# The order of small steps around TensorE in a two-layer attention and gMLP kernel: keys' sum, block sums, early transposes, row statistics

## The chip, the cores and the metric

The kernel runs on one core of a Trainium2 chip. TensorE (PE) multiplies matrices and writes into PSUM banks; VectorE (DVE), ScalarE (ACT) and GpSimd (POOL) do the element-wise work; SyncE (SP) issues all DMA transfers. Each engine works through its own instructions in the order in which the program issued them, and semaphores hold an instruction back until what it needs is there. The metric is the device time of one execution in microseconds, the median of several runs.

## The reference

Four residual blocks follow each other on x (2048 rows of 512), all in float32: attention A, mixer B, A, B, with the same weights in both layers.

```python
def _A_ref(x, wqkv, wo):                      # H = 32 heads of 16
    q, k, v = ...                             # from x @ wqkv
    phi = lambda t: jnp.where(t > 0, t + 1, jnp.exp(t)) + 1e-6
    pq, pk = phi(q), phi(k)
    kv = jnp.einsum("bhsd,bhse->bhde", pk, v)
    z = jnp.einsum("bhsd->bhd", pk)           # the keys' sum
    num = jnp.einsum("bhqd,bhde->bhqe", pq, kv)
    den = jnp.einsum("bhqd,bhd->bhq", pq, z)[..., None] + 1e-6
    return (num / den)... @ wo
...
def _B_ref(x, w_in, w_sp, b_sp, w_out):
    z = _gelu(jnp.einsum("bsd,df->bsf", x, w_in))
    z1 = z[..., :Fh]                          # Fh = 896
    z2 = _layernorm(z[..., Fh:], axis=-1)
    g = jnp.einsum("ts,bsf->btf", w_sp, z2) + b_sp[None, :, None]
    return jnp.einsum("bsf,fd->bsd", z1 * g, w_out)
...
x = x + _A_ref(_layernorm(x, axis=-1), A_wqkv, A_wo)
x = x + _B_ref(_layernorm(x, axis=-1), B_w_in, B_w_sp, B_b_sp, B_w_out)
...                                           # and both once more
```

## The kernel before, in words

The rows are cut into 16 tiles of 128. Every operand of a matmul is split into a high part (fp32r, made by an ACT copy, `high`, L119) and a low part (the rest, made by a DVE subtraction, `low`, L122), and each product is three matmuls: high by high, high by low, low by high (`mm3`, L133 to L135). So PE reads a low part only at its third matmul.

Per layer there are four stages, in this order:

- **P1** goes through the tiles i and makes keys and queries. Step s of `P1.run` works on several tiles at once: it loads x(s+3), takes row statistics of tile s+2 (`ln_a`: `stats` on DVE, L196 and L198, and three small POOL instructions, L200 to L203, of which the last makes `nb`), normalises tile s+2 on ACT (`ln_b`, L209), turns tile s (`T_high`, `T_low`), multiplies K of tile s-1 and Q of tile s-1 on PE, applies phi on ACT and DVE (`K_phi`, `Q_phi`, L327 to L329), splits x and the keys of tile s-1 (`xsplit`; `K_split`, L340 and L341) and accumulates G of tile s-2 (`Gmm`). Q of the last six tiles is put off (`late`) into the following stage. A side queue splits one piece of a further weight per step. `Turn` turns a tile in one of two ways: by four PE transposes into a PSUM bank (L221), for the tiles in `by_pe` (0, 1, 2 in the first layer, 10 to 15 in both), or by a store of the tile as `xt` to DRAM and a reload with another layout (`turn.load`), followed by a DVE transpose within 32x32 blocks (L260).
- **The keys' sum** z is accumulated in `K_split` by a POOL add of two SBUF tiles (L346).
- **The block sums** (`Sums`) belong to a later stage, which multiplies by w_sp with seven block products instead of eight and needs sums of blocks of w_sp. `tick` stores the sums of the tick before, issues loads for the next, and has POOL add twice (L788). There are 32 ticks, in the first layer alone: six in steps 2 to 7 of P1, the others in P2 and P4.
- **transition** and **P2**: the small products of attention; then per tile the product of pq and z on POOL (`a`, L567), the denominators (`a2_den`, L579 to L581), their product with pq (`a2_mul`, L588, and in the first tiles a copy on ACT, L240), turning (`b_high`, `b_low`), the matmul `c`, the residual add and row statistics (`c2`), store and normalise (`c3`), turning again (`d_high`, `d_low`), and the products of the mixer (`e`, `f`). Steps 1 to 4 turn by PE and carry the deferred Q.
- **P4** multiplies by w_sp and by w_out; `o(i)` makes output tile i and `zsplit(i)` its operand. In the first layer `join` puts the start of the next layer's P1 beside it: loads, statistics, and the splits of wk and wq.

There is no planner: the order is the one written out in the code. SBUF tiles come from queues of fixed slots: 22 pages of 128x512 floats (`pages`), larger `quads` and `bigs`, and eight PSUM banks. `get` takes the slot that has been free longest (`popleft`, L41), `put` adds one at the end (L50). A slot is given back when the instruction that reads it last is issued, and the next one to write it waits on a semaphore for that reader.

Of the kernel before, what the change touches and what calls it, by code (L numbers as in the profile page):

```python
# [13 lines left out]
OP = mybir.AluOpType  # L14
# [5 lines left out]
NT = S // P  # L20
# [51 lines left out]
def mixer_kernel(ctx: ExitStack, tc: tile.TileContext, x_in, wqkv, wo_d, win1_d, win2_d, wsp_d, bsp_d, wout_d,  # L72
# [192 lines left out]
    class P1:  # L265
# [71 lines left out]
        def K_split(self, i):  # L337
            r = self.r.pop(i)
            h, l = pages.get(PAGE, F32R), pages.get(PAGE, F32R)
            nc.scalar.activation(h, r, AF.Copy, bias=PHI_EPS)  # L340
            nc.vector.scalar_tensor_tensor(l, r, PHI_EPS, h.bitcast(F32), op0=OP.add, op1=OP.subtract)  # L341
            self.pk[i] = (h, l)
            if i == 0:
                self.zacc = r
            else:
                nc.gpsimd.tensor_tensor(self.zacc, self.zacc, r, op=OP.add)  # L346
                pages.put(r)

        def Q(self, i):
            self.qb = self.proj(i, self.wq)  # L350
# [78 lines left out]
        def run(self, sums):  # L429
            side = deque()  # L430
            for w in (self.wv, self.wo, self.win2):
                side.extend([w] * len(w.pieces))
            side[0].fetch()
            ND = NT - DEFER
            for s in range(1, NT + 2):
                self.loadx(s + 3)
                self.turn.load(s + 1)
                if 2 <= s < NT:
                    self.T_high(s)
                if s == 1:  # L440
                    if not self.kb:
                        self.K(0)
                    self.K(1)
                elif 2 < s <= NT:
                    self.K(s - 1)
                self.ln_a(s + 2)
                if 2 <= s < NT:
                    self.T_low(s)
                if s <= NT:
                    self.K_phi(s - 1)  # L450
                if s <= ND:
                    self.Q(s - 1)
                if s == NT + 1:
                    self.late()
                if s <= NT:
                    self.xsplit(s - 1)
                    self.K_split(s - 1)
                self.ln_b(s + 2)
                if s <= ND:
                    self.Q_phi(s - 1)  # L460
                if s >= 2:
                    self.Gmm(s - 2)
                if s == NT + 1:
                    self.late_phi()
                if self.L == 0 and s == 2:
                    sums.slots = Sheets(bigs, 2)
                if self.L == 0 and 2 <= s < 8:
                    sums.tick(s < 7)
                if self.L == 0 and s == 8:
                    sums.store()  # L470
                    sums.slots.close()
                    sums.slots = pages
                if side:
                    side.popleft().piece()
                if side:
                    side[0].fetch()
            while side:
                side.popleft().piece()


    def transition(p1, p2):
        wv, wo = p1.wv, p1.wo
        zh, zl = pages.get(PAGE, F32R), pages.get(PAGE, F32R)
        za = p1.zacc
        nc.vector.tensor_scalar(za, za, NT * PHI_EPS, None, op0=OP.add)
        split(zh, zl, za, True)
        pages.put(za)
        p1.late()
        p1.wk.free()
        g = (quads.get([P, 4, 512], F32R), quads.get([P, 4, 512], F32R))  # L490
        for c in range(4):
            split(g[0][:, c, :], g[1][:, c, :], p1.G[c])
            banks.put(p1.G[c])
        zb = banks.get(PAGE)
        nc.tensor.matmul(zb, ones, zh, start=True, stop=False)
        nc.tensor.matmul(zb, ones, zl, start=False, stop=True)
        pages.put(zh, zl)
        p2.zbc = pages.get(PAGE)
        nc.scalar.activation(feats(p2.zbc, True), feats(zb, False), AF.Copy)
        banks.put(zb)  # L500
        p2.a(0)
        p1.late_phi()
        p2.win1.fetch()
        p2.win1.fetch()
        p2.zeps = small.tile([P, 32], F32, name="zeps", bufs=1)
        nc.vector.tensor_reduce(p2.zeps, p2.zbc.rearrange("p (h d) -> p h d", d=16), axis=mybir.AxisListType.X,
                                op=OP.add)
        nc.vector.tensor_scalar(p2.zeps, p2.zeps, PHI_EPS, PHI_EPS, op0=OP.mult, op1=OP.add)

        p2.a2_den(0)  # L510
        m = pages.get([P, 4, P])
        for q in range(4):
            b = banks.get([P, P])
            s = slice(q * P, (q + 1) * P)
            for c in range(4):
                mm3(b, (wv.h[:, c, s], wv.l[:, c, s]), (g[0][:, c, s], g[1][:, c, s]), c == 0, c == 3)
            nc.vector.tensor_mul(m[:, q, :], b, mask)
            banks.put(b)
        kvh, kvl = pages.get([P, 4, P], F32R), pages.get([P, 4, P], F32R)
        for q in range(0, 4, 2):  # L520
            split(kvh[:, q:q + 2, :], kvl[:, q:q + 2, :], m[:, q:q + 2, :])
        pages.put(m)
        quads.put(*g)
        wv.free()
        p2.a2_mul(0)
        p2.a(1)
        p1.late()
        p2.a2_den(1)
        p2.W2 = (quads.get([P, 4, 512], F32R), quads.get([P, 4, 512], F32R))
        for q in range(4):  # L530
            b = banks.get(PAGE)
            mm3(b, (kvh[:, q, :], kvl[:, q, :]), (wo.h[:, q, :], wo.l[:, q, :]), True, True)
            split(p2.W2[0][:, q, :], p2.W2[1][:, q, :], b)
            banks.put(b)
            if q == 1:
                p2.b(0)
        pages.put(kvh, kvl)
        wo.free()
        p2.a(2)
        p1.late_phi()  # L540
        p2.a2_mul(1)
        p1.late()
        p2.a(3)
        p2.a2(2)
        p1.late_phi()


    class P2:
# [69 lines left out]
        def c2(self, i):  # L618
            x = self.x[i]
            nc.vector.tensor_add(x, x, self.cb)  # L620
            banks.put(self.cb)
            self.ms[i] = stats(x, 1)

        def c3(self, i):
            x = self.x.pop(i)
# [75 lines left out]
        def run(self, sums):  # L701
            w1 = self.win1
            for s in range(1, NT + 3):
                self.loadx(s + 1)
                self.qturn.load(s + 1)
                if s in self.qturn.by_pe:
                    self.c(s - 1)
                    self.b_high(s)
                    self.c2(s - 1)
                    self.b_low(s)  # L710
                    if s >= 2:
                        self.d_high(s - 2)
                        self.d_low(s - 2)
                    self.p1.late()
                    self.c3(s - 1)
                    self.a2(s + 2)
                    self.p1.late_phi()
                    self.a(s + 3)
                else:
                    if s < NT:  # L720
                        self.b_high(s)
                    self.a2_den(s + 2)
                    if s < NT:
                        self.b_low(s)
                    if s <= NT:
                        self.c(s - 1)
                        self.c2(s - 1)
                    if s == NT:
                        quads.put(*self.W2)
                        pages.put(self.zbc)  # L730
                    self.a2_mul(s + 2)
                    late = s - 2 in self.xturn.by_pe
                    if late:
                        self.d_high(s - 2)
                        self.d_low(s - 2)
                    if s <= NT:
                        self.c3(s - 1)
                    self.a(s + 3)
                    if s <= NT + 1 and not late:
                        self.d_high(s - 2)  # L740
                        self.d_low(s - 2)
                if s >= 4:
                    self.e4(s - 4)
                self.xturn.load(s - 1)
                if s >= 3:
                    self.e(s - 3)
                    self.e2(s - 3)
                    self.e3(s - 3)
                self.f()
                self.f()  # L750
                self.fq.extend(self.fnext)
                self.fnext = []
                w1.piece(True)
                w1.fetch()
                if s > 7:
                    sums.tick()
                if s >= NT + 1:
                    self.p4.fetch(s - NT - 1)
# [53 lines left out]
    class P4:  # L812
# [243 lines left out]
        def join(self, i, nxt):  # L1056
# [9 lines left out]
            if i in (11, 12):  # L1066
                nxt.turn.load(i - 11)
            if 10 <= i < 14:
                nxt.wk.piece()
                nxt.wq.piece()  # L1070
            if i == 14:
                nxt.T(0)
            if i == 15:
# [47 lines left out]
```

## Time and profile before

| | us |
|---|---|
| median of 3 runs | 1407.29 (1407.14 to 1407.45) |
| the profiled execution | 1407.07 |
| its span in the profile | 1405.3 |
| PE busy | 1394.3 (99%) |
| DVE busy | 889.5 (63%) |
| ACT busy | 572.7 (41%) |
| POOL busy | 405.8 (29%) |

All times below are microseconds from the start of the span. In the first layer P1 runs from about 10 to 132, the transition to about 152, P2's first steps follow; the second layer's P1 begins at about 707 and its P2 at about 848. A row of the timeline gives start, duration, engine, line, operation, the tiles written and read, and in brackets the idle time before it and what ended that. A PE matmul's end is modelled and overlaps the next, so spacing of starts says when PE stood still.

### The profile page before, as it was taken

The page shows a single profiled execution, that of the slowest core. Times are in us where ns is not written, and L with a number is a line of the kernel's source. Part 1 is how long each engine was busy: PE and PEld are TensorE (multiplying, and loading weights), DVE is VectorE, ACT ScalarE, POOL GpSimd, SP SyncE. Part 2 cuts the span into 40 slices and gives each one's busy share as a digit, 9 for nine tenths or more (in the row PEclk, how much of TensorE's full clock was granted, in tenths as well). Part 3 has the DMA queues.
Part 4 walks back from the last instruction along what each step waited for, and adds up shares of the span by engine and source line. Part 5 has one row for each costly group of instructions (what it writes and reads, how often), then busy time and mean ns, then how long its engine had stood idle before and what let it go on. Part 6 is the DMA issues. An engine that isn't in the chain of part 4 may idle for free.

```text
span 1405.3 us, 17490 instructions
## 1 busy us (share of the span) xinstructions
PE 1394.3 (99%) x6318; PEld 1167.0 (83%) x6318; DVE 889.5 (63%) x1263; ACT 572.7 (41%) x871; POOL 405.8 (29%) x490
## 2 busy tenths in 40 slices
PE   9999999999999999999999999999999999999998
PEld 7788888888888888888888888888888888888887
DVE  7876786753587666583578767766415466666632
ACT  5665544434322332351366655444333233333420
POOL 3843244544366002040023334432100030022300
PEclk9999999999999999999999999999999999999999
DMA  5831156766887433443644212555335344434432
GB/s 198 258 117 46 56 177 213 258 226 204 326 299 265 133 121 136 167 163 120 210 127 142 61 38 93 183 177 163 114 119 158 105 165 134 130 120 169 152 112 90
DMA packets 134390, 219.39 MB, mean 156 GB/s; under 512 B 11552, under 2 KB 44064, under 8 KB 134304
## 3 DMA queue, kind: packets, MB, share of 16 engines
q1 hardware_dynamic: 134304, 218.28, 47.5%
q8 instruction: 49, 0.80, 0.2%
q14 instruction: 37, 0.30, 0.1%
HBM read 153.49 MB, written 64.75 MB: 155 GB/s over the span
## 4 chain that ended last, share of the span: by engine, by line
PE 93%; DVE 2%; ACT 1%; DMA 1%; POOL 1%; issue 1%; SPq 0%; ACTq 0%; DVEq 0%; POOLq 0%
PE bank L135 18%; PE bank L134 18%; PE bank L133 18%; PE bank L908 13%; PE bank L910 13%; PE bank L909 13%; PE bank L221 1%; DMA pg<-in_wqkv_dram 1%; DVE qd L122 0%; DMA pg<-in_x_dram 0%; DVE st L196 0%; DVE pg L588 0%; ACT z_q L328 0%; ACT pg L209 0%; ACT z_q L327 0%
## 5 line engine op out<-in xcount | busy, mean ns | idle before, releaser
L908 PE MATMUL bank<-qd,pg 128*128 128x512 f32 x800 | 311.3, 389 | 0.0
L910 PE MATMUL bank<-qd,pg 128*128 128x512 f32 x800 | 311.2, 389 | 0.0
L909 PE MATMUL bank<-qd,pg 128*128 128x512 f32 x800 | 311.2, 389 | 0.0
L847 DVE TENSOR_TENSOR qd<-qd,qd 128x1024 fp32r<-128x1024 f32 x112 | 151.9, 1356 | 175.6 <-ACT qd L846 175.4
L846 ACT ACTIVATE qd<-qd 128x1024 fp32r<-128x1024 f32 x112 | 118.5, 1058 | 215.8 <-PE bank L910 195.5
L935 POOL TENSOR_TENSOR bg<-bg,pg 128x512 f32<-128x512 f32 x56 | 85.5, 1562 | 408.8 <-DVE bg L962 195.5
L910 PEld LDWEIGHTS bank<-qd,pg 128*128 128x128 f32 x800 | 150.2, 188 | 31.3
L908 PEld LDWEIGHTS bank<-qd,pg 128*128 128x128 f32 x800 | 150.1, 188 | 31.3 <-DVE bg L953 0.2
L909 PEld LDWEIGHTS bank<-qd,pg 128*128 128x128 f32 x800 | 150.2, 188 | 31.2
L135 PE MATMUL bank<-qd,pg 128*128 128x512 f32 x384 | 150.7, 392 | 3.0 <-DVE pg L122 3.0
L200 POOL TENSOR_SCALAR rs<-mv 128x1 f32<-128x1 f32 x96 | 33.1, 344 | 378.8 <-DVE mv L198 378.3
L209 ACT ACTIVATE pg<-pg,nb,rs 128x512 f32<-128x512 f32 x63 | 51.0, 810 | 181.2 <-POOL nb L203 181.2
L133 PE MATMUL bank<-qd,pg 128*128 128x512 f32 x288 | 112.7, 391 | 1.4 <-ACT pg L119 1.4
L134 PE MATMUL bank<-qd,pg 128*128 128x512 f32 x288 | 112.3, 390 | 0.0
L133 PE MATMUL bank<-bg,qd 128*128 128x448 f32 x256 | 94.0, 367 | 0.0
L134 PE MATMUL bank<-bg,qd 128*128 128x448 f32 x256 | 93.6, 366 | 0.0
L135 PE MATMUL bank<-bg,qd 128*128 128x448 f32 x256 | 93.4, 365 | 0.0
L788 POOL TENSOR_TENSOR pg<-pg,pg 128x512 f32<-128x512 f32 x52 | 78.0, 1499 | 47.3 <-DMA pg<-in_wsp_dram 33.8
L135 PEld LDWEIGHTS bank<-qd,pg 128*128 128x128 f32 x384 | 72.1, 188 | 21.2 <-DVE pg L122 6.4
L135 PE MATMUL bank<-qd,bg 128*128 128x512 f32 x224 | 87.5, 390 | 0.0
L135 PE MATMUL bank<-wo,qd 128*128 128x512 f32 x224 | 87.3, 390 | 0.2 <-DVE qd L122 0.2
L134 PE MATMUL bank<-qd,bg 128*128 128x512 f32 x224 | 87.4, 390 | 0.0
(128 smaller groups left out, 2640.2 us busy)
## 6 DMA issues: line engine op xcount, KB each, us to landing
qd<-s SPq DMA_DIRECT2D x64, 512.0 KB, 3.3
qd<-in_wsp_dram SPq DMA_DIRECT2D x48, 512.0 KB, 4.0
pg<-x SPq DMA_DIRECT2D x64, 256.0 KB, 3.0
z<-pg SPq DMA_DIRECT2D x56, 256.0 KB, 2.3
pg<-z SPq DMA_DIRECT2D x56, 256.0 KB, 5.3
pg<-in_wsp_dram SPq DMA_DIRECT2D x52, 256.0 KB, 4.8
s<-pg SPq DMA_DIRECT2D x52, 256.0 KB, 4.5
x<-pg SPq DMA_DIRECT2D x48, 256.0 KB, 2.6
```

The lines of the kernel that those rows point to most:

```text
L133: nc.tensor.matmul(out, ah, bh, start=start, stop=False)
L134: nc.tensor.matmul(out, ah, bl, start=False, stop=False)
L135: nc.tensor.matmul(out, al, bh, start=False, stop=stop)
L200: nc.gpsimd.tensor_scalar(rs, mv[:, 1:2], LN_EPS, None, op0=OP.add)
L209: nc.scalar.activation(y, x, AF.Identity, bias=nb, scale=rs)
L788: nc.gpsimd.tensor_tensor(t, a, b, op=OP.add)
L846: nc.scalar.activation(w[:, 0], r, AF.Copy)
L847: nc.vector.tensor_sub(w[:, 1], r, w[:, 0].bitcast(F32))
L908: m(out, h[:, o], w[:, 0, j, :], start=start, stop=False, skip_group_check=True)
L909: m(out, h[:, o], w[:, 1, j, :], start=False, stop=False, skip_group_check=True)
L910: m(out, l[:, o], w[:, 0, j, :], start=False, stop=stop, skip_group_check=True)
L935: nc.gpsimd.tensor_tensor(u, u, z1, op=OP.mult)
```

## The change

Six edits, all of them of order:

1. `K_split`: the POOL add writes its sum into the tile r of the newest keys, which `K_split` also reads for the low part (L341), and gives back the page of the old sum. Before, it wrote into the old sum and gave back r.
2. `P1.run`, first layer: a tick of the block sums is issued directly behind `ln_a(s+2)` instead of at the end of the step, and the first loads of blocks are issued in step 1.
3. `P1.run`: a tile in `by_pe` is turned in the step before, between `K_split(s-1)` and `ln_b(s+2)`.
4. `transition`: `late_phi` is issued between the denominators and the product of tile 2.
5. `P2`: in steps 1 to 4 the statistics behind the residual add (`c_stats`) are issued behind `b_low`; in the other steps nothing moves.
6. `join`: turns 10 and 11 split two pieces of wk each, 12 and 13 two of wq; before, each turn split one of both.

```diff
@@ K_split
-                nc.gpsimd.tensor_tensor(self.zacc, self.zacc, r, op=OP.add)
-                pages.put(r)
+                nc.gpsimd.tensor_tensor(r, self.zacc, r, op=OP.add)
+                pages.put(self.zacc)
+                self.zacc = r
@@ P1.run
-                if 2 <= s < NT:
+                turned = 2 <= s < NT and s not in self.turn.by_pe
+                if turned:
                     self.T_high(s)
...
                 self.ln_a(s + 2)
-                if 2 <= s < NT:
+                if self.L == 0 and s == 1:
+                    sums.slots = Sheets(bigs, 2)
+                    sums.fetch()
+                if self.L == 0 and 2 <= s < 8:
+                    sums.tick(s < 7)
+                if turned:
                     self.T_low(s)
...
                     self.K_split(s - 1)
+                if s + 1 < NT and s + 1 in self.turn.by_pe:
+                    self.T(s + 1)
                 self.ln_b(s + 2)
...
-                if self.L == 0 and s == 2:
-                    sums.slots = Sheets(bigs, 2)
-                if self.L == 0 and 2 <= s < 8:
-                    sums.tick(s < 7)
@@ transition
-        p2.a2(2)
+        p2.a2_den(2)
         p1.late_phi()
+        p2.a2_mul(2)
@@ P2
             banks.put(self.cb)
-            self.ms[i] = stats(x, 1)
+
+        def c_stats(self, i):
+            self.ms[i] = stats(self.x[i], 1)
...
                     self.b_high(s)
                     self.c2(s - 1)
                     self.b_low(s)
+                    self.c_stats(s - 1)
...
                         self.c2(s - 1)
+                        self.c_stats(s - 1)
@@ join
             if 10 <= i < 14:
-                nxt.wk.piece()
-                nxt.wq.piece()
+                for _ in range(2):
+                    (nxt.wk if i < 12 else nxt.wq).piece()
```

## The prediction

> **What bounds the kernel now.** I read the page first, for the share of each engine and the clock:
>
> ```profile
> span 1405.3 us, 17490 instructions
> PE 1394.3 (99%) x6318; PEld 1167.0 (83%) x6318; DVE 889.5 (63%) x1263; ACT 572.7 (41%) x871; POOL 405.8 (29%) x490
> PEclk9999999999999999999999999999999999999999
> ```
>
> TensorE is busy throughout, at the full clock. Only time in which it waits can be won. The view of waits names waiters, but its idle time is measured from a modelled end, so I took the waits from the timeline of PE by spacing of starts: undisturbed 128x512 matmuls start every 0.23 us (22.69, 22.92).
>
> ```profile
> 22.92 0.39 PE L134 MATMUL bank<-qd,pg 128*128 128x512 f32 x1
> 23.83 0.50 PE L135 MATMUL bank<-qd,pg 128*128 128x512 f32 x1 [0.52 <-DVE pg L122]
> ...
> 41.40 0.50 PE L133 MATMUL bank<-qd,pg 128*128 128x512 f32 x1 [1.40 <-ACT pg L119]
> ...
> 156.19 0.50 PE L135 MATMUL bank<-qd,pg 128*128 128x512 f32 x1 [0.72 <-DVE pg L122]
> ...
> 163.40 0.50 PE L135 MATMUL bank<-qd,pg 128*128 128x512 f32 x1 [0.53 <-DVE pg L122]
> ```
>
> Each such start is late, and the next follows after 0.34 instead of 0.23. Lateness plus that 0.11 gives, at these four, 0.79, 1.94 (three starts suffer), 0.99 and 0.80; the second layer has 0.44 (692.56), 0.26 (709.87), 0.99 (851.11) and 0.79 (858.32). Together 7.0 us: the most that any reordering can win.
>
> The fourth view is the timeline of DVE and POOL in a step with block sums (step 4 of the first P1):
>
> ```profile
> 43.14 0.68 DVE L122 TENSOR_TENSOR pg<-pg,pg 128x512 fp32r<-128x512 f32 x1
> 43.92 1.60 DVE L341 SCALAR_TENSOR_TENSOR pg<-pg,pg 128x512 fp32r<-128x512 f32 x1
> ...
> 46.39 0.85 DVE L122 TENSOR_TENSOR qd<-pg,qd 128x512 fp32r<-128x512 f32 x1
> 47.16 1.09 DVE L260 STREAM_TRANSPOSE pg<-pg 128x512 f32<-128x512 f32 x1
> ```
> ```profile
> 42.90 0.26 POOL L203 TENSOR_SCALAR nb<-mv,rs 128x1 f32<-128x1 f32 x1
> 43.30 1.67 POOL L346 TENSOR_TENSOR pg<-pg,pg 128x512 f32<-128x512 f32 x1
> 44.94 3.46 POOL L788 TENSOR_TENSOR bg<-bg 128x512 f32<-128x512 f32 x2
> ```
>
> A DVE instruction with two SBUF operands and a POOL add don't run together: L341 takes 1.60 here and 0.69 where POOL is idle (713.49). Its last 0.55 come after the add's end at 44.97, and the adds in turn take 1.67 to 1.74 instead of 1.29 (36.48). Three adds and three such DVE instructions take turns: 5.2 us from the end of nb (43.16) to 48.40, the same 5.2 to 5.3 in steps 5, 6 and 7.
>
> **The change, part by part.** Sums go against the profiled execution's own 1407.07 us, 0.2 under the median 1407.29.
>
> Join pieces. The wait at 692 (0.44) comes from ACT, which stood at the first piece of wq until its load landed (683.54, then 689.55), with zsplit behind it. wk's four pieces, fetched two turns earlier, are now split first; wq's loads, issued until 686.9, are needed two turns (9.5 us) later. Gain 0.44; the same eight splits run. The 0.26 at 709 is a chain from the last o to T(1) and stays.
>
> Early T. T(2) keeps its place on PE (after Q(0), at 16.78), but its high (0.60) and low (0.66) move from behind ln_a(4) and its statistics to behind K_split(0): low done near 20.5 instead of 23.77, needed at 23.1. The 0.79 goes. ACT's ln_b(3), its xt store on SP and the reload are 0.5 later; the reload landed at 27.0 and is used at 28.26, which covers it. T(10) to T(15) of both layers: PE's four transposes (0.44) stand ahead of Gmm instead of behind it, same count. The tightest input is x(13), normalised until 98.07, 0.6 later behind an ACT high; PE would ask near 100.4. Cost nothing, cover 1.7.
>
> First block sums. Three loads (256 KB each) go out at about 10 instead of 26.33; SP there waits until 19.87 anyway. The last load before them lands at 14.4, and landings follow each other by 0.7, so they land by 16.6. The sums no longer hold up the row statistics (POOL waited for that load, and the statistics of 30.04 got nb only at 35.27). The 1.94 goes. In steps 2 to 7 the sums' two stores and up to three loads now stand on SP ahead of xt's store. They wait for the adds of the step before, which end about when SP gets there (46.7 against 47.9 in step 5), and xt's store comes only at 52.19; at 0.7 each the five transfers are through by then, and the reload has 2.2 of cover (landed 52.5, used 54.72). Cost nothing.
>
> Keys' sum. Now it writes the page that L341 reads, so POOL waits for L341. Behind step 8 and in layer 1 this only frees L341 (1.60 to 0.69); PE doesn't wait there, so it is worth nothing. The transposes of the next step start 1.0 after the later sum's end (sum to about 724.0, L260 at 725.07).
>
> But in steps 2 to 7 of layer 0 the order on POOL becomes statistics, two block sums, keys' sum. Who waits for the keys' sum? K_split gives back a page when it is issued. Counted through the code, a step begins with 9 free pages; up to that point it takes 10 and returns 5, so 4 stand ahead in the queue, and the next takers are ln_b's y, the side weight's load, loadx, turn.load's tile and then, fifth, the tile that DVE's transpose L260 of the next step writes. In the trace's operands L260 of steps 3 to 8 indeed waits on the semaphore that L346 and L788 raise. Today L346 is first of the three adds and done at 44.97, 2.2 before L260. After the change it is last, done 5.2 after nb, while L260 would start 4.0 after nb: 1.3 late. Behind L260 on DVE stand ln_a and T_low; POOL's next statistics wait for ln_a. So it is a loop: L260 to the next nb 3.57 (47.16 to 50.73), nb to the last add 5.2, a step to L260 0.05: 8.84 per step, against 7.55 today (47.16 to 54.72) and PE's 36 matmuls x 0.2267 = 8.16. Bounds for such a period: three undisturbed adds, 3.57 + 3.9 = 7.5, no loss; the slowest seen, 8.9. I take 8.84, as the same six instructions took 5.2 in all four steps.
>
> First pass, step 2: nb(4) at 25.05, L341(1) to 25.62, sums to 28.0, L122 and keys' sum to 29.7. L260(3) at 29.75 (28.26 today), T_low(3) 2.5 later at 32.2. K(3), no longer held up, wants it at 31.31: 0.94 + 0.11 = 1.05 lost. Then five steps (K(4) to K(8)) at 8.84 - 8.16 = 0.68 to 0.71: 3.5. New loss 4.6; bounds 0.3 (only a first collision) and 5.0.
>
> Start of P2, both layers. PE waited for b_low(1) (L122 at 155.48) behind residual 0.68, statistics 0.70 + 0.18, and late_phi behind a2_mul(2). New order on DVE: den(2) to 150.70, late_phi's L329 when ACT is through (151.40), a2_mul(2), residual to 153.3, low at 154.0 to 154.65; c(1) wants it at 155.31. The 0.99 goes. ACT's copy of q(2) is 1.3 later (153.4) and PE wants it at 157.6. The statistics now end at 155.4 (155.56 today), normalised y(0) at 157.6; PE transposes it at 158.0. Second wait: a2_mul(3), L588, starts 1.25 behind the statistics' end (L579 0.09 before that end, 1.33 through the three den instructions, as 149.41 to 150.74), POOL's a(4), L567, 1.29 behind it (155.56 to 156.85). Today L588 started later and lost the port:
>
> ```profile
> 156.85 1.30 POOL L567 TENSOR_TENSOR pg<-z_q,pg 128x512 f32<-128x512 f32 x1
> ```
> ```profile
> 157.38 1.32 DVE L588 SCALAR_TENSOR_TENSOR pg<-z_q,den 128x512 f32<-128x512 f32 x1
> ```
>
> If L588 goes first, low(2) is done at 161.2 and wanted at 161.67: the 0.80 goes too. If L567 goes first, low(2) comes at 162.3, and 0.77 and up to 0.1 at the next transposes stay. The nearest row is step 4, where L567 started at 179.94, L588 at 179.99, and L588 took 1.79: the earlier starter won by 0.05. Here DVE is earlier by 0.04, so I take it as winner. In steps 3 and 4 the same swap is covered: e's 24 matmuls stand ahead of c. Gain 0.99 + 0.80 + 0.99 + 0.79 = 3.57; bounds 1.8 and 3.57. The Trainium skill, page "SBUF — State Buffer", section "Who interferes with whom", says that issue order decides who blocks, and for the whole instruction; by this rule the result is the sum below, while going by who won in the two rows it would be that of the second rival.
>
> Sum: -0.44 - 0.79 - 1.94 - 3.57 + 4.6 = -2.1, so 1404.9 on the profiled execution's scale, 1405.1 as a median.
>
> **The rivals.** (1) The page's wait doesn't bind: POOL's adds finish before L260, or another tile gets the page. For it: undisturbed adds need 3.9, and the wait is hidden today. Against: 5.2 in four steps of four. Loss 0.3 instead of 4.6: 1400.8.
> (2) POOL wins the port in P2's second step in both layers: 0.35 gained in all (2.1 less 2 x 0.88), 1406.9. For it: a margin of 0.04 and two rows in which it won; against: the order of starts.
> (3) Slower: early T holds up ACT. When ACT has caught up (K_phi at 94.66 right after its matmuls), T_high waits for PE's transposes and delays ln_b by up to 1.2; where Q is deferred (steps 12 to 14, 5.9 us each) PE asks for x one Gmm (2.7) sooner. It decides once ln_b is later than today by more than the 1.7 above. Six steps of up to 1.2: 7.2, so 1412.3. Against: the transposes there end 0.4 after K, before ACT gets through K_split.
> (4) The change doesn't free L341 in steps 2 to 7, as a block sum now holds the port; this is in my sum and moves nothing further.
>
> **How the numbers follow.** My forecast 0.54, of which a sixth lies above a gain of 2.8 (0.2%, about what a measurement of this kernel tells from no change); rival 1 0.18; rival 2 0.21; rival 3 0.07. Faster by over 0.2%: 0.18 and 0.09, so 0.27; slower 0.07; within 0.66. The range reaches from rival 1, 1400.8, to 1407.6, rival 2 with the loop at its upper bound 5.0 and 0.3 of spread; out of it are rival 3 and the tails, about 0.15. My forecast's own range is 1404.2 to 1406.0.
>
> **What would show it.** Right: no late start near 22.9, 155, 162, 692, 850 and 857; in the first P1 six late matmuls, one per step from about 31 to 75, released by DVE L122, L260 8.8 apart and starting at the end of an L346; L341 at 0.69 in layer 1. Wrong: L260 8.2 or less apart (rival 1), L588 near 1.9 at about 156.7 (rival 2), late transposes L221 between 84 and 115 (rival 3), or late starts anywhere else.

## The result and the profile after

The changed kernel takes 1405.39 us (median of 22 runs, 1404.91 to 1405.90), the kernel before 1407.45 beside it (22 runs). The ratio is 0.9984, with a 95% interval of 0.9978 to 0.9991: 2.06 us won, 0.15%. That is little, but the interval doesn't reach 1, and the slowest run after (1405.90) is faster than the fastest before (1407.14). The forecast was 1405.1, range 1400.8 to 1407.6.

The profiled execution took 1405.06 (before 1407.07). Its page:

```profile
span 1403.3 us, 17509 instructions
PE 1395.3 (99%) x6318; PEld 1166.9 (83%) x6318; DVE 875.1 (62%) x1263; ACT 571.9 (41%) x871; POOL 399.4 (28%) x490
PEclk9999999999999999999999999999999999999999
```

TensorE is as busy as before and the clock is full. DVE and POOL lost 14.4 and 6.4 us of busy time although the change removes no instruction of theirs; they block each other less. That alone brings nothing, as neither is the bound. What counts is late starts on PE. Lateness is counted as in the prediction, spacing less 0.227, summed over each late start and the starts behind it that follow after 0.33 to 0.39: 7.01 before, 5.26 after. Left out are 19 spacings of 0.31 to 0.32 in each of the two profiles. The late starts after, in the timeline of PE (start, duration, and in brackets the idle time and what ended it):

```profile
31.75 0.50 PE L133 MATMUL bank<-qd,pg 128*128 128x512 f32 x1 [0.52 <-ACT pg L119]
...
40.71 0.50 PE L133 MATMUL bank<-qd,pg 128*128 128x512 f32 x1 [0.23 <-ACT pg L119]
41.05 0.40 PE L134 MATMUL bank<-qd,pg 128*128 128x512 f32 x1
41.44 0.50 PE L135 MATMUL bank<-qd,pg 128*128 128x512 f32 x1
41.78 0.40 PE L133 MATMUL bank<-qd,pg 128*128 128x512 f32 x1
...
49.71 0.50 PE L133 MATMUL bank<-qd,pg 128*128 128x512 f32 x1 [0.24 <-ACT pg L119]
```

What the second group waits for, in the timelines of ACT and DVE:

```profile
40.03 0.63 ACT L119 ACTIVATE pg<-pg 128x512 fp32r<-128x512 f32 x1 [3.42 <-DVE pg L260]
```
```profile
40.69 0.69 DVE L122 TENSOR_TENSOR pg<-pg,pg 128x512 fp32r<-128x512 f32 x1
```

The first matmul of a group waits for the high part, done at 40.66, right behind L260's tile. The third, L135 at 41.44, waits for the low part, done at 41.38, and that wait ends last.

Three more groups follow at 58.69, 67.65 and 76.64, and a single late start at 710.11. The start at 31.75 is 0.91 behind its predecessor, the next five 0.62 to 0.65; the three starts behind each follow after 0.34, 0.39 and 0.34 instead of 0.23. That is 1.07 + 0.77 + 0.78 + 0.80 + 0.78 + 0.80 = 5.0, and 0.26 at 710. The waits of before near 23, 41, 156, 163, 692, 851 and 858 are gone; near 41 the shorter one of the second group stands in place of the old one. So 6.75 us were taken out, and 5.0 put in: 1.75 less. The last matmul starts 1.63 earlier (1399.13 against 1400.76); the remaining 0.35 of the profiled 2.0 lies behind the last matmul, which is 4.15 from the end of the span here and 4.50 before. In the other profiles of this study that distance is 4.15, 4.5 or 4.6 without relation to the edits, so it isn't the change's.

Why the six starts are late: timelines of DVE and of POOL, first at the first tick of block sums, then in step 4. L798 is the block sum (L788 before); the other lines up to L346 have their old numbers.

```profile
27.69 1.08 DVE L122 TENSOR_TENSOR qd<-pg,qd 128x512 fp32r<-128x512 f32 x1
29.95 1.08 DVE L260 STREAM_TRANSPOSE pg<-pg 128x512 f32<-128x512 f32 x1 [1.19 <-POOL pg L346]
...
42.45 1.84 DVE L122 TENSOR_TENSOR pg<-pg,pg 128x512 fp32r<-128x512 f32 x1
44.21 1.79 DVE L341 SCALAR_TENSOR_TENSOR pg<-pg,pg 128x512 fp32r<-128x512 f32 x1
...
46.53 1.46 DVE L122 TENSOR_TENSOR qd<-pg,qd 128x512 fp32r<-128x512 f32 x1
47.91 1.08 DVE L260 STREAM_TRANSPOSE pg<-pg 128x512 f32<-128x512 f32 x1
```
```profile
28.17 1.75 POOL L346 TENSOR_TENSOR pg<-pg,pg 128x512 f32<-128x512 f32 x1
...
42.22 0.27 POOL L203 TENSOR_SCALAR nb<-mv,rs 128x1 f32<-128x1 f32 x1
42.44 3.01 POOL L798 TENSOR_TENSOR bg<-bg 128x512 f32<-128x512 f32 x2
46.15 1.29 POOL L346 TENSOR_TENSOR pg<-pg,pg 128x512 f32<-128x512 f32 x1 [0.70 <-DVE pg L341]
```

At the first tick L260 stands 1.19 and starts 0.03 behind the end of the keys' sum (29.92): the wait for the page, as forecast. In step 4 L260 waits for nothing of POOL's: it follows the L122 ahead of it on DVE, 0.47 after the keys' sum has ended at 47.44. What is slow there is the six instructions themselves. The first block sum starts 0.01 ahead of the L122 of `xsplit` and blocks it (1.84 instead of 0.68); the second (43.82 to 45.45) blocks L341 (1.79); the keys' sum, which now must wait for L341 (POOL stands 0.70), blocks the L122 of the weight's split (1.46). Each DVE instruction ends 0.55 behind the add that blocks it. From the end of nb (42.49) to L260 that makes 5.42, from L260 to the end of the next nb (51.48) 3.57, together 8.98, and PE's matmuls of a step take 8.16.

In the second step of P2 DVE came first at the port by 0.07, and POOL's add paid (timelines of DVE and POOL; L594 was L588, L573 was L567):

```profile
159.26 0.69 DVE L594 SCALAR_TENSOR_TENSOR pg<-z_q,den 128x512 f32<-128x512 f32 x1
```
```profile
159.33 1.75 POOL L573 TENSOR_TENSOR pg<-z_q,pg 128x512 f32<-128x512 f32 x1
```

The second layer has the same, 851.82 against 851.89. No late start is left near 156, 163, 851 or 858.

### The profile page after: what moved, and what is told of

It reads as the page before. It is cut to its first block, busy times and chain, and to the rows that moved or that the text cites. A ratio compares the mean times of both kernels' runs of the same rounds, so it can differ in the third digit from the quotient of the medians.

```text
span 1403.3 us, 17509 instructions
## 1 busy us (share of the span) xinstructions
PE 1395.3 (99%) x6318; PEld 1166.9 (83%) x6318; DVE 875.1 (62%) x1263; ACT 571.9 (41%) x871; POOL 399.4 (28%) x490
## 4 chain that ended last, share of the span: by engine, by line
PE 94%; DVE 3%; ACT 1%; POOL 1%; issue 1%; DMA 0%; SPq 0%; DVEq 0%; POOLq 0%
PE bank L135 18%; PE bank L134 18%; PE bank L133 18%; PE bank L920 13%; PE bank L919 13%; PE bank L918 13%; PE bank L221 1%; DVE pg L122 1%; DVE pg L260 0%; DMA pg<-in_x_dram 0%; SPq L115 0%; DVE pg L341 0%; DVE bg L122 0%; DVE pg L329 0%; ACT pg L328 0%
## 5 line engine op out<-in xcount | busy, mean ns | idle before, releaser
L135 PE MATMUL bank<-qd,pg 128*128 128x512 f32 x384 | 150.6, 392 | 0.0
L135 PE MATMUL bank<-bg,qd 128*128 128x448 f32 x256 | 93.4, 365 | 0.0
L798 POOL TENSOR_TENSOR pg<-pg,pg 128x512 f32<-128x512 f32 x52 | 79.0, 1520 | 46.4 <-DMA pg<-in_wsp_dram 30.7
L135 PE MATMUL bank<-qd,bg 128*128 128x512 f32 x224 | 87.5, 390 | 0.0
L134 PE MATMUL bank<-qd,bg 128*128 128x512 f32 x224 | 87.4, 390 | 0.0
L133 PE MATMUL bank<-qd,bg 128*128 128x512 f32 x224 | 87.2, 389 | 0.0
L135 PEld LDWEIGHTS bank<-qd,pg 128*128 128x128 f32 x384 | 72.1, 188 | 18.2 <-DVE pg L122 3.4
```

What stands on the lines that cost most here:

```text
L133: nc.tensor.matmul(out, ah, bh, start=start, stop=False)
L134: nc.tensor.matmul(out, ah, bl, start=False, stop=False)
L135: nc.tensor.matmul(out, al, bh, start=False, stop=stop)
L798: nc.gpsimd.tensor_tensor(t, a, b, op=OP.add)
```

## The experiments

Two theories were set against each other for the six late starts. The page: L260 writes the page that the keys' sum gives back, so it can't start before that sum has ended, wherever the sum stands. The port, as what DVE and POOL can't use at once is called here: three POOL adds and three DVE instructions with two SBUF operands take turns, and L260 comes behind them whatever page it writes. Diffs are against the changed kernel unless said otherwise; each time stands beside runs of the kernel before on the same chip (1407.3 to 1407.5).

**The old sum's page given back at the end of the step.** L260 then gets another page, and everything else stays.

```diff
-                pages.put(self.zacc)
+                self.zold = self.zacc
...
+                if self.zold is not None:
+                    pages.put(self.zold)
+                    self.zold = None
```

> The changed kernel, but the old sum's page is given back at the end of the step instead of in K_split, so that the next step's DVE transpose takes another page. Page theory (the prediction's): the transposes L260 wait for the keys' sum because of the page; without it the six late starts of the first P1 (5.0 us in the changed kernel's profile) go but for some 0.3, 1400.7. Port theory (from the changed kernel's profile): only the first transpose, at 29.95, waited for the page; from step 4 on it starts behind the weight split L122, which took 1.45 instead of 0.68 because the keys' sum held the port. Then only the first late start (1.07) goes, L260 stays 8.97 apart, and the time is 1404.2.

Measured: 1404.71, ratio 0.9982 (0.9973 to 0.9991). The first L260 comes at 28.26 instead of 29.95, and the late start near 31.7 is gone. The others stay, only later: 48.19 (0.69), 57.24, 66.27, 75.30, and a small one near 39.5. L260 is 9.02 to 9.06 apart. Its step 4, timelines of DVE and POOL (lines shifted by one, L802 is the block sum):

```profile
40.90 1.83 DVE L122 TENSOR_TENSOR pg<-pg,pg 128x512 fp32r<-128x512 f32 x1
42.66 1.78 DVE L342 SCALAR_TENSOR_TENSOR pg<-pg,pg 128x512 fp32r<-128x512 f32 x1
...
44.96 1.46 DVE L122 TENSOR_TENSOR qd<-pg,qd 128x512 fp32r<-128x512 f32 x1
46.34 1.08 DVE L260 STREAM_TRANSPOSE pg<-pg 128x512 f32<-128x512 f32 x1
```
```profile
40.89 2.99 POOL L802 TENSOR_TENSOR bg<-bg 128x512 f32<-128x512 f32 x2
44.58 1.28 POOL L347 TENSOR_TENSOR pg<-pg,pg 128x512 f32<-128x512 f32 x1 [0.70 <-DVE pg L342]
```

The same collisions in the same durations without the page. So the page explains the first late start alone; the period is the port's. The gain over the changed kernel (0.7 in the medians, 1.2 in lateness: 4.03 against 5.26) is that first wait.

**The block sums back at the end of the step**, behind the keys' sum; their first loads stay in step 1, the keys' sum keeps its new form.

```diff
@@ behind ln_a
-                if self.L == 0 and 2 <= s < 8:
-                    sums.tick(s < 7)
@@ end of the step
+                if self.L == 0 and 2 <= s < 8:
+                    sums.tick(s < 7)
```

> The changed kernel, but the ticks of the block sums stand at the end of the step again, behind the keys' sum; the first loads stay in step 1. Both theories: the keys' sum is the first of the three adds, done long before the next transpose, and of the three adds only one stands ahead of the weight split; L260 about 8.0 apart, less than PE's 8.16, so nearly all 5.0 us of late starts go: 1400.4 to 1401. A rival (the block sums themselves are too much for POOL and DVE wherever they stand): 1404 or more.

Measured: 1400.71, ratio 0.9953 (0.9940 to 0.9965), 4.7 below the changed kernel. L260 is 8.18 to 8.20 apart, at PE's pace; of the six late starts one of 0.34 at 31.93 is left. Step 5, DVE and POOL:

```profile
49.77 0.69 DVE L341 SCALAR_TENSOR_TENSOR pg<-pg,pg 128x512 fp32r<-128x512 f32 x1
...
52.23 1.48 DVE L122 TENSOR_TENSOR bg<-pg,bg 128x512 fp32r<-128x512 f32 x1
53.63 1.09 DVE L260 STREAM_TRANSPOSE pg<-pg 128x512 f32<-128x512 f32 x1
```
```profile
48.76 0.27 POOL L203 TENSOR_SCALAR nb<-mv,rs 128x1 f32<-128x1 f32 x1
50.61 1.30 POOL L346 TENSOR_TENSOR pg<-pg,pg 128x512 f32<-128x512 f32 x1 [1.59 <-PE bank L135]
51.86 1.30 POOL L798 TENSOR_TENSOR bg<-bg 128x512 f32<-128x512 f32 x1
53.24 1.63 POOL L798 TENSOR_TENSOR bg<-bg,bg 128x512 f32<-128x512 f32 x1
```

Only one of the three DVE instructions is blocked ahead of L260 instead of three; the second sum runs beside L260 and the statistics. From the end of nb (49.03) to L260 it is 4.60 instead of 5.42. So the loss comes from where the block sums stand. This profile also has one late start of 1.03 at 237, in P2, on which more below.

**The block sums' place alone** (the kernel before with edit 2).

```diff
@@ before, P1.run
                 self.ln_a(s + 2)
+                if self.L == 0 and s == 1:
+                    sums.slots = Sheets(bigs, 2)
+                    sums.fetch()
+                if self.L == 0 and 2 <= s < 8:
+                    sums.tick(s < 7)
...
-                if self.L == 0 and s == 2:
-                    sums.slots = Sheets(bigs, 2)
-                if self.L == 0 and 2 <= s < 8:
-                    sums.tick(s < 7)
```

> The kernel before with the block sums' edit alone (first loads in step 1, ticks behind the row statistics; the keys' sum and everything else as before). Port theory: the position of the ticks is enough for the loss; L260 8.7 apart as in the run with the old keys' sum, which left P1 1.07 later than before at its end: 1408.4. If the loss needs the keys' sum's wait as well, only the gain of the early loads is left, 1.94: 1405.4.

Measured: 1407.89, ratio 1.0003 (0.9994 to 1.0012). The wait of before at 41.4 is gone, and five groups of late starts (40.05, 48.73, 57.43, 66.11, 74.81) of 0.5 each are there, though the keys' sum has its old form and waits for nothing. L260 is 8.68 to 8.72 apart. Edit 2 alone takes as much as it gives.

**The keys' sum in its old form**, all else changed.

```diff
-                nc.gpsimd.tensor_tensor(r, self.zacc, r, op=OP.add)
-                pages.put(self.zacc)
-                self.zacc = r
+                nc.gpsimd.tensor_tensor(self.zacc, self.zacc, r, op=OP.add)
+                pages.put(r)
```

> The changed kernel with the keys' sum written into the old sum as before, so that POOL doesn't wait for L341. If the position of the block sums alone makes the loss, it stays: 1405.4. If the wait for L341 adds to it (in the changed kernel's step 4 the keys' sum starts 0.7 after the second block sum's end, at 46.15 instead of at once), the period falls by some 0.3 to 8.7 and the time to 1404.0.

Measured: 1404.21, ratio 0.9977 (0.9968 to 0.9986), 1.2 below the changed kernel. L260 is 8.69 to 8.70 apart, 0.28 less than after, and the late starts are smaller. In its step 4 the keys' sum starts right behind the second block sum, instead of standing 0.70 for L341 (timeline of POOL, L797 is the block sum):

```profile
42.07 3.00 POOL L797 TENSOR_TENSOR bg<-bg 128x512 f32<-128x512 f32 x2
45.04 1.74 POOL L346 TENSOR_TENSOR pg<-pg,pg 128x512 f32<-128x512 f32 x1
```

In late starts of the first P1 it is 2.8 against 5.0, with 0.78 near 240 besides that the changed kernel's profile doesn't have. So the wait that edit 1 adds costs 1.2 us by the medians, up to 2.2 by the late starts.

**Block sums last and the old keys' sum**, that is, edit 1 undone and edit 2 cut down to the early first loads.

```diff
-                nc.gpsimd.tensor_tensor(r, self.zacc, r, op=OP.add)
-                pages.put(self.zacc)
-                self.zacc = r
+                nc.gpsimd.tensor_tensor(self.zacc, self.zacc, r, op=OP.add)
+                pages.put(r)
...
-                if self.L == 0 and 2 <= s < 8:
-                    sums.tick(s < 7)
...
+                if self.L == 0 and 2 <= s < 8:
+                    sums.tick(s < 7)
```

> The changed kernel with the ticks at the end of the step again and the keys' sum written into the old sum as before; the first loads stay in step 1. Port theory: the keys' sum needn't wait for L341 and all three adds end sooner before the weight split, so L260 is 7.6 apart (8.19 with the keys' sum's new form), nothing else is won since PE doesn't wait there: 1400.6. If the new form of the keys' sum brings PE something, this is slower than 1400.7 by more than the spread.

Measured: 1400.36, ratio 0.9951 (0.9938 to 0.9963), the best of the study: 7.15 below the kernel before. Of 7.0 us of lateness 0.5 is left, the 0.26 that was to stay (705.39) and one start at 398.65. A step of it, DVE and POOL (L797 is the block sum):

```profile
47.65 1.60 DVE L341 SCALAR_TENSOR_TENSOR pg<-pg,pg 128x512 fp32r<-128x512 f32 x1
...
50.12 0.84 DVE L122 TENSOR_TENSOR bg<-pg,bg 128x512 fp32r<-128x512 f32 x1
50.88 1.08 DVE L260 STREAM_TRANSPOSE pg<-pg 128x512 f32<-128x512 f32 x1
```
```profile
47.04 1.67 POOL L346 TENSOR_TENSOR pg<-pg,pg 128x512 f32<-128x512 f32 x1
48.66 1.75 POOL L797 TENSOR_TENSOR bg<-bg 128x512 f32<-128x512 f32 x1
50.49 1.63 POOL L797 TENSOR_TENSOR bg<-bg,bg 128x512 f32<-128x512 f32 x1
```

L341 is blocked here (1.60) and free in the run with the new keys' sum (0.69), and the times are the same within their spread, 1400.36 and 1400.71. So the shorter L341 is worth nothing to PE here. L260 is 7.55 to 7.56 apart, as forecast, but for one distance of 8.92: there a block sum starts 0.03 ahead of the weight's split (58.04 against 58.07), which then takes 1.81. PE isn't late even behind that one.

**P2's edits alone** (the kernel before with edits 4 and 5), **and edit 5 alone**.

```diff
@@ transition, in the first of the two only
-        p2.a2(2)
+        p2.a2_den(2)
         p1.late_phi()
+        p2.a2_mul(2)
@@ P2, steps 1 to 4, in both
                     self.c2(s - 1)
                     self.b_low(s)
+                    self.c_stats(s - 1)
```

> The kernel before with the two edits of transition and P2 alone (late_phi between den and product of tile 2; statistics behind b_low). The prediction's step: all four late starts of P2 go, 3.57, nothing else moves: 1403.8. If one of the later steps takes a part back (the transposes of y, c(2)), 1404.5 to 1406.

> The kernel before with the statistics behind b_low alone. From the rows of before: b_low(1) would be done at 155.2 and is wanted at 155.31, so the first late start of each layer goes (0.99); the loop to b_low(2) starts 0.55 later than with late_phi moved too, so low(2) comes at 161.9 where 161.67 is wanted, and some 0.3 of the second stays: 1407.4 - 2 x 1.5 = 1404.4. If late_phi's place does the work, 1407.4 or little under it.

Measured: both edits 1403.46, ratio 0.9973 (0.9962 to 0.9983); edit 5 alone 1404.84, 0.9982 (0.9973 to 0.9991). In the profile with both the last matmul starts 3.5 earlier than before, at an equal distance from the end of the span, and the forecast was 3.57. With edit 5 alone the start of P2 gains 1.13 in the first layer and 1.31 in the second, against 1.81 and 1.85 with both. The place of `late_phi` is therefore worth about 0.6 per layer. What is left with edit 5 alone isn't at `c(2)`, where it was expected, but at PE's transposes (eight of them take 1.25 at 157.56, 1.04 in the kernel before).

**POOL made to win the port in P2's second step**, by delaying DVE: a write of a constant tile between the denominators and the product with pq in step 1, once, and then three times.

```diff
-                    self.a2(s + 2)
+                    self.a2_den(s + 2)
+                    if s == 1:
+                        for _ in range(3):
+                            nc.vector.memset(ones_f, 1.0)
+                    self.a2_mul(s + 2)
```

> The changed kernel with one more DVE instruction (a memset of 128x128, 0.17 where it stands at the start of the run) between the denominators and the product of tile 3 in step 1 of P2, in both layers. If the port's order decides (L594 started 0.07 ahead of POOL's L573 and won), POOL now starts first, L594 takes about 1.8, and PE waits about 0.8 at c(2) in each layer: 1407.0. If the order doesn't matter, the 0.2 disappear in the cover: 1405.4.

> As the run with one memset, with three (each added some 0.08, since they overlap, and one left L594 0.05 ahead of L573). L594 should now start about 0.1 behind L573. If the order at the port decides, L594 takes 1.8, low(2) is 1.3 later, and PE waits about 0.8 at c(2) and up to 0.2 at the transposes in each layer: 1407.0. If the order doesn't matter, 1405.2.

Measured: with one write 1405.13, ratio 0.9986 (0.9977 to 0.9995), and no answer: the write (0.17) overlaps its neighbours and L594 starts at 158.53, still 0.05 ahead of L573 at 158.58. With three, 1407.4, ratio 1.0000 (0.9991 to 1.0009). Timelines of DVE, POOL and PE with three:

```profile
158.87 0.68 DVE L728 MEMSET ones_f<- 128x128 f32 x3
159.47 1.37 DVE L594 SCALAR_TENSOR_TENSOR pg<-z_q,den 128x512 f32<-128x512 f32 x1
```
```profile
159.00 1.29 POOL L573 TENSOR_TENSOR pg<-z_q,pg 128x512 f32<-128x512 f32 x1
```
```profile
163.71 0.50 PE L133 MATMUL bank<-qd,pg 128*128 128x512 f32 x1
164.04 0.40 PE L134 MATMUL bank<-qd,pg 128*128 128x512 f32 x1
164.62 0.50 PE L135 MATMUL bank<-qd,pg 128*128 128x512 f32 x1 [0.18 <-DVE pg L122]
```

Now POOL starts first, by 0.47 and not by the 0.1 expected. Its add takes 1.29, L594 takes 1.37 (1.8 expected) and ends 0.55 behind the add, and PE is late at 163.71 and 164.62, and again at 857.91 and 858.83. The whole gain is gone, 2.0 in the medians. The writes put L594's start off by 0.54 (0.39 behind L587's start it would be 158.93), but not its end: that hangs on POOL's add, which the writes don't move. So the price is that of the order at the port.

**Early turning.** Edit 3 alone on the kernel before, and the changed kernel with only T(2) early.

```diff
@@ edit 3 alone, on the kernel before
-                if 2 <= s < NT:
+                turned = 2 <= s < NT and s not in self.turn.by_pe
+                if turned:
...
+                if s + 1 < NT and s + 1 in self.turn.by_pe:
+                    self.T(s + 1)
@@ only T(2) early, on the changed kernel
-                turned = 2 <= s < NT and s not in self.turn.by_pe
+                turned = 2 <= s < NT and (s > 2 or s not in self.turn.by_pe)
...
-                if s + 1 < NT and s + 1 in self.turn.by_pe:
+                if s == 1 and s + 1 in self.turn.by_pe:
```

> The kernel before with the early turning of PE's tiles alone. Additive reading (the prediction's sum): the late start at 23.83 goes and no other changes, 0.79 gained, 1406.6. Chain reading: the late start at 41.40 is set by the load, the sums and the statistics ahead of T(4), not by PE, so PE only arrives there sooner and waits 0.79 longer (2.7 instead of 1.94): 1407.4, no gain. A third: late starts near 84 to 115 if the early transposes hold up ACT, 1408 or more.

> The changed kernel with only tile 2 turned early; tiles 10 to 15 are turned where they were before. The prediction's step: their early turning is covered and worth nothing, 1405.2, no late starts between 84 and 126 in either kernel. Rival 3 of the prediction (early T holds up ACT): faster than the changed kernel by up to some us.

Measured: edit 3 alone 1406.63, ratio 0.9996 (0.9987 to 1.0005), which the time can't tell from no change nor from 0.79 (the medians differ by 0.73). Its PE timeline:

```profile
41.30 0.50 PE L133 MATMUL bank<-qd,pg 128*128 128x512 f32 x1 [1.22 <-ACT pg L119]
```

The wait of before stays, and ends at 41.30 (41.40 before). In this profile the matmuls are still level with those of before at 188. Its last one is 0.41 earlier, and that comes at 692, where each profile without edit 6 has a wait, of 0.32 to 0.63 in spacing. In the profiles without edit 2 that start comes at 41.30 to 41.40 whether PE was late near 23.8 (before 0.68, edit 5 alone 0.26) or not (edit 3 alone, edits 4 and 5 alone): what PE gains earlier, it stands longer there. So the profiles show no gain from edit 3 without edit 2; the medians alone would fit either reading. The wait near 23.8 also depends on the start of the run: it is missing in two profiles without edit 3, in which the first K products began 0.8 to 0.9 later (8.44 and 8.57 against 7.67). Edit 3 alone began late too (8.70), so that profile doesn't show what took this wait away; the changed kernel's does, as it began early (7.52) and has none. Only T(2) early: 1405.39, ratio 0.9984 (0.9975 to 0.9993), the same as the changed kernel, and neither profile has a late start between 84 and 126. Early turning of tiles 10 to 15 neither costs nor brings anything.

**Late starts without relation to the edits.** Eight of the thirteen profiles have late starts with spacings of 0.35 to 1.03 near 237 to 241 or 398 to 405, the others have none there. No run was made on them, but the traces tell what those near 237 to 241 follow on: a block sum whose load lands late. In the run with the block sums last (POOL):

```profile
231.70 2.66 POOL L798 TENSOR_TENSOR pg<-pg,pg 128x512 f32<-128x512 f32 x2 [6.24 <-DMA pg<-in_wsp_dram]
...
235.42 0.26 POOL L203 TENSOR_SCALAR nb<-mv,rs 128x1 f32<-128x1 f32 x1
```

The row statistics stand behind that sum, as they did before at 30, ACT's normalising waits for `nb`, and PE for ACT. In the three profiles with such a late start POOL stands 5.47 to 6.24 for that load, in the other ten 3.69 to 5.00. Why the load lands later in some executions is open. Near 398 to 405 PE's weight load waits 0.4 to 0.6 for a DVE sum; why only in some executions is open too.

## Why the prediction was right, and where not

- **The total** (1405.1, measured 1405.39) came from two sums that both held: 6.74 to be removed, 6.75 removed; 4.6 to be added, 5.0 added. Of the 2.0 between the profiled executions 0.35 lies behind the last matmul and isn't the change's, so that it came so near the forecast 2.1 is in part luck.
- **Join pieces** (0.44): the wait at 692 is gone, and so it is in every profile that has edit 6, while all profiles without it have one (0.32 to 0.63 of spacing). It was not timed alone.
- **Early T** (0.79): gone in the changed kernel, but the step treated it as a gain of its own. By the profiles it is one only because edit 2 removes the wait behind it. The cost of nothing for T(10) to T(15) held.
- **First block sums** (1.94): gone. The three early loads and the SP queue delayed nothing that PE showed.
- **P2** (3.57): 3.5 in the run with these two edits alone. The choice that DVE wins the port was right (0.07 ahead, forecast 0.04); the price of the other order is 2.0 in the medians (1407.4 less 1405.4) where the second rival had 2 x 0.88 = 1.76.
- **Keys' sum**: this is the step with the wrong mechanism. The prediction said that L260 "waits for the keys' sum" through the page, in every step. That was so once: with the page out of the way the first late start went and the period stayed at 9.0. The loop was right, its lower half too (3.57 forecast, 3.57 measured), and so was "the same six instructions"; but L260 is tied to them through DVE's own queue. The size was right by luck, for a neighbouring reason: the six instructions bind through DVE's queue at nearly the time at which they would have bound through the page (the sum ends 0.5 ahead of L260). The low part was to come late by 0.94 in the first group, and L135 there starts 0.95 late (32.47 against 31.52, three undisturbed spacings behind 30.84), though the matmul that stands still first is the one that needs the high part. The term that was mis-sized is the six instructions, 5.2 taken from before (with 3.57 and 0.05 that makes 8.82, written as 8.84), 5.42 measured: the order of starts at the port isn't that of before, since DVE's first instruction lost it by 0.01, and the keys' sum stands 0.70 for L341. A period of 8.98 instead of 8.84 makes 0.79 per step instead of 0.70.
- **Rivals.** The first (the page doesn't bind, 0.3 lost) tied the whole loss to the page; the run with the other page shows the page gone and the loss there. The second has its price but not its order. The third didn't come. The fourth, that L341 isn't freed in steps 2 to 7, is what happened in steps 3 to 7 (1.78 to 1.79); in step 2 and in the second layer L341 takes 0.69.

The Trainium skill, page "SBUF — State Buffer", section "Who interferes with whom", says that a DVE instruction with two SBUF inputs contends with a GpSimd one that reads SBUF, and that issue order decides who blocks. The traces agree at every collision shown here, going by the order of starts: in P2's second step 0.07 ahead left L594 at 0.69, and 0.47 behind made it 1.37.

## What to carry to other kernels

Where TensorE is busy 99% of the span, count its late starts, and treat the waits of one chain as a whole: a gain ahead of a wait that ends at a fixed time is only waited away there. Before long adds are moved on POOL, write down both engines' instructions between two fixed points (here nb and the transpose) with the price of each collision, and put those adds last that nobody needs soon; that order alone was worth 4.7 us here. When a forecast names a wait, ask which instruction stands directly ahead on the same queue: it may be as late by itself, and removing the wait then brings nothing.

## What the runs showed of the hardware

- A lead of 0.01 went with who had the port for the whole add. POOL ahead (42.44 against 42.45) made DVE's instruction take 1.84 instead of 0.68; DVE ahead at the changed kernel's first tick (24.99 against 25.00) left L341 at 0.69 and made the add take 1.83. Starts nearer still don't tell: in two other profiles L341 started less than 0.01 ahead and took 1.85 (late page, 24.78 for both; three writes, 24.96 against 24.97).
- A blocked DVE instruction ends 0.55 behind the end of the add that blocks it, at four different collisions (step 4's three and L594), although alone it needs 0.68 or 0.69.
- A 128x128 constant write of 0.17 on DVE put the next instruction off by 0.02 only (158.53, where 0.39 behind L587 is 158.51); three put it off by 0.54.
- The transposes within 32x32 blocks (1.09 beside an add of 1.63) and the row statistics (0.64) are not slowed by POOL's adds.
